# Routing attention into a cosine router on one core: early gathers held to their turns, four scatters moved behind the region, the last pair's groups summed in one visit

## The chip, the core and the metric

The kernel runs on one core of a Trainium2 chip. The metric is the time of one execution on the device in microseconds (us), as the median of several runs. The core has engines that each work through their own list of instructions in order: PE (TensorE; PEld is its weight load), DVE (VectorE), ACT (ScalarE), POOL (GpSimd) and SP (SyncE, which here only issues DMAs). They wait for each other by semaphores. All numbers below are of the kernel before the change.

## What is computed

```python
def attention(q, k, v, centroids):            # q, k, v: 4 x 8 x 768 x 64; centroids: 8 x 16 x 64
    q_assign = argmax(cosine(q, c), -1)       # each query and key belongs to one of 16 clusters
    k_assign = argmax(cosine(k, c), -1)
    mask = q_assign[:, :, :, None] == k_assign[:, :, None, :]
    scores = where(mask, q @ k.T / sqrt(64), -1e9)
    attn = exp(scores - max(scores))
    return (attn / (sum(attn) + 1e-9)) @ v

def router(x, expert_emb, tau, w1, w2):       # x: 3072 x 512; w1: 8 x 512 x 1024; w2: 8 x 1024 x 512
    logits = cosine(x, expert_emb) / tau
    expert_idx = argmax(logits, 1)
    gate = softmax(logits)[arange(N), expert_idx]
    for e in range(8):
        mask = expert_idx == e
        out[mask] = gate[mask, None] * (relu(x[mask] @ w1[e]) @ w2[e])

x = attention(...).transpose(0, 2, 1, 3).reshape(3072, 512)
out = router(x, ...)
```

Everything is float32. Each token goes to a single expert, so the tokens of one expert have to be gathered, multiplied, and scattered back.

## The kernel before

**Attention.** The 4 batches and 8 heads are worked off as 16 pairs n of two heads (four pairs to a batch, b and nb). A pair has two groups (the halves of the 768 queries), a group has six units, and one iteration `it` of the main loop (0 to 5 within a pair) does two units. For a unit, `scores` (line 571) multiplies a block of keys with the queries, together with a small product of one-hot cluster codes that does the masking; `expo` (582, ACT) makes `prob`; `attend` (593, PE) multiplies it with v, and DVE adds it up into `acc` (602, 612). The scores of a unit are issued one iteration ahead of its `attend`.

After a pair come its denominators and its x. `total` (643) multiplies `acc` with ones on PE, which sums over the keys. Called with two groups it uses tiles of 32 output rows and 192 columns, transposes the sums on DVE (660), takes the reciprocal of few elements (661) and lets POOL spread them with eight copies (664). Called with one group it uses 64 rows and 384 columns, and DVE takes the reciprocal of 128x384 directly (652). `divide` transposes the spread reciprocals back (675, two groups only) and makes `xT` (679). `rows` transposes xT (696) and stores it into the DRAM tensor `x_rows` with four DMAs from SP (703). All pairs but the last do this with both groups at once, in the next pair's iterations. The last pair calls each of `total`, `divide`, `rows` and `products` once for each group: the first group within the pair, the second in the tail behind it. `products` (722, PE) multiplies xT with the expert embeddings, `logits` (734, DVE) transposes the result, `choose` finds each token's expert, with a running sum `cumx` on POOL (776).

**Experts.** The tokens of one expert are cut into items. Four items, `E0[0]` to `E0[3]`, are "early": blocks of 128 tokens of earlier batches, whose tables are made during the last two batches. Behind them come the items of `later`, alternately "block" (128 tokens) and "sized" (160 to 272 tokens). For an item, POOL gathers the rows of x with four indirect DMAs (1144, one for each quarter), `turn_x` transposes them (1262 on DVE; 1269 with eviction 1272 on ACT for E0[0]), `hidden` multiplies by w1 in two halves of 16 matmuls (1386, evicted by ACT at 1393; sized items at 1293 and 1300), `result` multiplies by w2 (1426, evicted at 1437), and POOL scatters the rows to `out_dram` (1155). Early items also gather their gates (`fetch_gate`, tile gatein). The weights have two slots for w1 and two for w2; SP loads 2 MB at a time (1194), the first loads in halves of 1 MB.

**What sets the order.** Each engine's list is written out by hand: the instructions stand in the order in which the Python code issues them. The table `early` names, by batch, pair and iteration, what is put into the main loop. For the gathers of E0[1] and E0[2] it says:

```python
(3, 3, 2): lambda: early_lot(1, 2),
(3, 3, 3): lambda: early_lot(1, 1),
(3, 3, 4): lambda: early_lot(1, 1),
(3, 3, 5): lambda: early_lot(2, 1),
```

`early_lot(j, n, behind)` issues the next n gathers of item j. With `behind`, POOL first copies one element of that tile, so that the gathers behind it on POOL can't go before the tile is written. The calls in the loop have no `behind`; those in the tail copy an element of a `hT`.

The tail behind the main loop runs on PE in this order: products of the last pair's first group, half of E0[0]'s hidden, `total` of the second group, the other half, products of the second group, E0[1]'s hidden, `ranks` (858, 865), result of E0[0], and on.

In the last loop, over `later`, scatters and gathers lie in a list `queue` with a due item. `pump(n, behind)` issues the next n; `share` issues as many as are needed to have those that are due issued in time. Between the halves of the result of item LAST-2 stands `overflow()`, a region under `tc.If` (1732) that is run only if more blocks are needed than planned. The six scatters of the sized item LAST-3 are due at LAST-2, and are issued before and at this region.

Of the kernel before, what the change touches and what calls it, by code (L numbers as in the profile page):

```python
# [9 lines left out]
F32 = mybir.dt.float32  # L10
# [8 lines left out]
P = 128  # L19

SQ = 32
# [18 lines left out]
def kernel(  # L40
# [590 lines left out]
    def total(*gs):  # L631

        g = gs[0]
        d = gr[g]
        n = units[GU * g][0]
        G = len(gs)
        bk = misc()

        M, W = (D, HS) if G == 1 else (D // 2, HS // 2)
        for i in range(P // M):  # L640
            for k, g in enumerate(gs):
                c = i * W % HS
                nc.tensor.matmul(
                    bk[M * i : M * i + M, W * k : W * k + W],
                    lhsT=ones[:, 0:M],
                    rhs=gr[g]["acc"][:, i * W // HS, c : c + W],
                    start=True,
                    stop=True,
                )
        den = d["den"] = smp.tile([P, G, HS], F32, tag="den", name="den", bufs=1)  # L650
        if G == 1:
            nc.vector.reciprocal(den[:, 0], bk[:, 0:W])
            return


        U = W // SQ
        sums = smp.tile([P, G * U, SQ], F32, tag="sums", name="sums", bufs=1)
        inv = smp.tile([P, G, U], F32, tag="inv", name="inv", bufs=1)
        inv2 = d["inv2"] = smp.tile([P, G, 2, U], F32, tag="inv2", name="inv2", bufs=1)
        nc.vector.transpose(sums.rearrange("p g i -> p (g i)"), bk[:, 0 : G * W])  # L660
        nc.vector.reciprocal(inv.rearrange("p k u -> p (k u)"), sums[:, :, 0])  # L661
        for i in range(4):
            for to in (i, i ^ 1):
                nc.gpsimd.tensor_copy(  # L664
                    inv2[M * to : M * to + M, :, i % 2], inv[M * i : M * i + M]
                )

    def divide(*gs):
        n, hq, _ = units[GU * gs[0]]
        d = gr[gs[0]]  # L670
        G = len(gs)
        if hq == 0:
            xT[pairs[n]] = xp.tile([P, 2, HS], F32, tag="xT", name="xT", bufs=4)
        if G == 2:
            nc.vector.transpose(
                d["den"].rearrange("p k (u t) -> p (k u) t", t=SQ),
                bc(d["inv2"].rearrange("p k h u -> p (k h u)"), [P, G * HS // SQ, SQ], 2),
            )
        nc.vector.scalar_tensor_tensor(
            out=xT[pairs[n]][:, hq : hq + G],  # L680
            in0=ld[n]["o_sum"][:, hq : hq + G, 0:HS],
            scalar=ld[n]["o_sum"][:, hq, HS:HE],
            in1=d["den"],
            op0=ALU.add,
            op1=ALU.mult,
        )
        for g in gs:
            gr[g].clear()
# [680 lines left out]
    def flat(t):  # L1369
        return t.rearrange("p k w -> p (k w)")  # L1370

    def hidden(it, halves=(0, 1)):

        d = mo[it]
        for half in halves:
            if half == 0:
                d["hT"] = (
                    flat(szp.tile([P, KF, max(CAPS)], F32, tag="hTs", name="hTs", bufs=1))[:, 0:F]
                    if it.kind == "whole"
                    else mop.tile([P, F], F32, tag="hT", name="hT")  # L1380
                )
            f0 = 512 * half
            bk = psH.tile([P, 512], F32, tag="h_ps", name="h_ps")
            for m in range(0, 512, P):
                for c in range(KD):
                    nc.tensor.matmul(  # L1386
                        bk[:, m : m + P],
                        lhsT=w1s[it.slot][:, c, f0 + m : f0 + m + P],
                        rhs=d["xT"][:, P * c : P * c + P],
                        start=(c == 0),  # L1390
                        stop=(c == KD - 1),
                    )
            nc.scalar.activation(d["hT"][:, f0 : f0 + 512], bk, ACTF.Relu)  # L1393

    def result_last(it):

# [18 lines left out]
    def result(it, halves=(0, 1)):  # L1415
# [44 lines left out]
        (3, 2, 3): lambda: fetch(E0[0]),  # L1460
        (3, 2, 5): lambda: order_x(E0[0]),
        (3, 3, 1): pa.spread_pieces,
        (3, 3, 2): lambda: early_lot(1, 2),
        (3, 3, 3): lambda: early_lot(1, 1),
        (3, 3, 4): lambda: early_lot(1, 1),
        (3, 3, 5): lambda: early_lot(2, 1),
    }
    early_jobs = {}

    def early_lot(j, n, behind=None):  # L1470

        if j not in early_jobs:
            early_jobs[j] = fetches(E0[j])
        if behind is not None:
            nc.gpsimd.tensor_copy(pace, behind)
        for job in early_jobs[j][0:n]:
            job()
        del early_jobs[j][0:n]
# [81 lines left out]
    with tc.manual_schedule(engines=by_hand):  # L1560
        begin()
        for i in range(0, len(units), 2):
# [14 lines left out]
                begun()  # L1577
                continue
            between(n, it)
            if it == 4 and n == NP - 1:  # L1580
                divide(2 * n)
            b, nb = divmod(n, NHP)
            if (b, nb, it) in early:
                early[b, nb, it]()
# [12 lines left out]
                unite(2 * n)  # L1597
            elif it == 5:
                unite(2 * n + 1)
            if i + 2 == len(units):  # L1600
                rows(ngroups - 2)
                route[b][0](0)
            if it == 0 and n > 0:
                total(2 * n - 2, 2 * n - 1)
            if it == 0 and n > 0:
                piece(n + 1, "products")
            if (nb, it) == (0, 4) and b > 0:
                route[b - 1][0](0, 1)
            if it == 3 and n == NP - 1:
                total(2 * n)  # L1610
        at.close()
        mop = ctx.enter_context(tc.tile_pool(name="mop", bufs=2, **tile_waits))
        rtb = ctx.enter_context(tc.tile_pool(name="rtb", bufs=1, **tile_waits))
# [8 lines left out]
        pb = Places(1, rtb)  # L1622
        gates = gate_pieces(0, B - 1)
        gates[0]()
        early_lot(2, 1)
        logits(0)
        hidden(E0[0], (0,))
        turn_x(E0[1])
        early_lot(2, 2, mo[E0[0]]["hT"][0:1, 511:512])
        total(ngroups - 1)  # L1630
        divide(ngroups - 1)
        ato.close()
        psY = ctx.enter_context(tc.tile_pool(name="psY", bufs=1, space=PSUM, reuse_waits="tile"))
        rows(ngroups - 1)
        gates[1]()
        gates[2]()
        hidden(E0[0], (1,))
        turn_x(E0[2])
        gates[3]()
        early_lot(3, 2, mo[E0[0]]["hT"][0:1, F - 1 : F])  # L1640
        weights1(E0[2])
        read(0, NJ, P - SQ, P)
        products(1)
        hidden(E0[1], (0,))
        logits(1)
        choose()
        early_lot(3, 2, mo[E0[1]]["hT"][0:1, 511:512])
        hidden(E0[1], (1,))
        weights1(E0[3])
        pb.ranks()  # L1650
        pb.firsts()
        for it in E0:
            fetch_gate(it)
        result(E0[0], (0,))
        pb.dest(0)
        pb.dest(1)
        result(E0[0], (1,))
        weights2(E0[2])
        pb.hot_blocks()
# [97 lines left out]
        for i, it in enumerate(later):  # L1757
# [8 lines left out]
            made = None  # L1766
            if i > 0 and later[i - 1].kind == "sized":
                made = mo[later[i - 1]]["ys"][0:1, 0, 0:1]
                queue.extend((min(i + 1, LAST - 2), f) for f in sends(later[i - 1]))
            if 0 < i < LAST - 1 and later[i + 2].kind == "sized":  # L1770
                jobs_of(later[i + 2], i)
            for k in range(i + 2, i + 4):
# [8 lines left out]
                    weights2(later[i + 2])  # L1781
                sized_result(it, lambda g, x: share(i, 3 - g, x) if g < 3 else None)
            elif i < LAST:
                share(i, 3, made)
                hidden(it, (0,))
                share(i, 2, mo[it]["hT"][0:1, 511:512])
                hidden(it, (1,))
                share(i, 1, mo[it]["hT"][0:1, F - 1 : F])
                if i == 0:
                    turn_x(later[1])  # L1790
                    pb.gates(slot_gates)
# [59 lines left out]
```

## Time and profile before

| what | us |
|---|---|
| median of 3 runs (698.12, 696.0, 698.7) | 698.12 |
| the profiled execution, whole | 695.11 |
| its span | 693.0 |
| clock of PE granted, mean | 0.998 |
| busy: DVE, ACT, POOL | 382.8, 262.2, 275.6 |
| POOL gathers (L1144), 56 | 56.8 |
| POOL scatters (L1155), 56 | 55.8 |
| moved by DMA | 135.55 MB, mean 196 GB/s |

The profile is of one execution. Times in it are counted from the start of its span; the execution as a whole took 2.1 us more. A line of the timeline gives start, duration, engine, source line, operation, output and inputs, and in brackets how long the engine sat idle before and what ended it. A line of the waits gives the total, the count and the longest. In the windows the DMA share is the mean busy share of the 16 DMA engines, and a number in brackets is a count of instructions. Rows of matmuls can lie over each other, as matmuls are pipelined: the distance to the next start is the better measure of what a group costs. Some matmul records can be missing.

The last attention pair lies at about 304 to 325 us, the tail with the early items from there to about 370, the region at 650.5, and the last scatter is issued at 688.69.

### The profile page before, as it was taken

What the parts mean: (1) busy time and instruction counts of PE and PEld (TensorE: products, weight loads), DVE (VectorE), ACT (ScalarE), POOL (GpSimd) and SP (SyncE); (2) the same over time, 40 slices, a digit from 0 to 9 for tenths busy, and PEclk for the clock granted to TensorE, in tenths of its full rate; (3) what the DMA queues carried; (4) which work ended last, traced back from release to release, by engine and by line L of the source; (5) the groups of instructions that cost most, each with busy time, mean ns of one, the idle gap of its engine ahead of it and who ended that gap; (6) DMA issues with size and microseconds to landing.
All of it is one profiled execution on the core that took longest, in us unless ns stands there. A gap on an engine that the chain in (4) does not pass through costs nothing. (4 is left out here: it accounts for less than half of the span.)

```text
span 693.0 us, 16339 instructions
## 1 busy us (share of the span) xinstructions
PE 682.6 (99%) x6521; PEld 460.4 (66%) x6521; DVE 382.8 (55%) x673; ACT 262.2 (38%) x444; POOL 275.6 (40%) x505
## 2 busy tenths in 40 slices
PE   8999999999999999999999999999999999999987
PEld 4544444444544444445866678888979797979785
DVE  6898998999899999997674122140301203030310
ACT  6665665576566765574242120101010101111011
POOL 2221222322131222343526343676756465647403
PEclk9999999999999999999999999999999999999999
DMA  9757755776678687689699957457787686878630
GB/s 147 121 82 116 114 100 86 153 141 106 108 131 163 139 147 142 171 209 292 175 311 388 372 189 268 147 175 279 281 282 280 202 301 231 306 249 310 242 133 33
DMA packets 244956, 135.55 MB, mean 196 GB/s; under 512 B 208640, under 2 KB 208642, under 8 KB 244876
## 3 DMA queue, kind: packets, MB, share of 16 engines
q1 hardware_dynamic: 238540, 121.29, 65.0%
q0 software_dynamic: 6160, 13.12, 5.6%
q8 instruction: 53, 0.87, 0.5%
q14 instruction: 27, 0.22, 0.1%
q10 hardware_dynamic: 176, 0.05, 0.0%
HBM read 115.93 MB, written 13.12 MB: 186 GB/s over the span
## 5 line engine op out<-in xcount | busy, mean ns | idle before, releaser
L582 ACT ACTIVATE prob<-s_ps 128x768 f32<-128x768 f32 x192 | 154.0, 814 | 104.7 <-PE s_ps L571 98.6
L571 PE MATMUL s_ps<-qT,kT 64*64 64x384 f32 x1536 | 156.9, 483 | 0.0
L593 PE MATMUL o_ps<-prob,v 64*64 64x385 f32 x1536 | 143.3, 484 | 0.6 <-issue 0.6
L612 DVE TENSOR_TENSOR acc<-acc,prob 128x768 f32<-128x768 f32 x128 | 121.5, 949 | 8.9 <-ACT prob L582 0.5
L593 PEld LDWEIGHTS o_ps<-prob,v 64*64 64x64 f32 x1536 | 58.6, 133 | 66.4 <-issue 58.1
L1340 DVE STREAM_TRANSPOSE ys<-y_ps 128x256 f32<-128x256 f32 (+4 forms) x16 | 6.1, 403 | 154.4 <-PE y_ps L1331 126.6
L1386 PEld LDWEIGHTS h_ps<-xTm,w1s 128*128 128x128 f32 x768 | 87.3, 192 | 2.0 <-issue 1.6
L1386 PE MATMUL h_ps<-xTm,w1s 128*128 128x128 f32 x768 | 88.3, 276 | 0.0
L571 PEld LDWEIGHTS s_ps<-qT,kT 64*64 64x64 f32 x1536 | 55.7, 133 | 35.9 <-issue 31.7
L1426 PE MATMUL y_ps<-w2s,hT 128*128 128x512 f32 x176 | 77.8, 594 | 0.3 <-PEq L1732 0.3
L1293 PE MATMUL h_ps<-xTs,w1s 128*128 128x272 f32 (+7 forms) x384 | 72.9, 346 | 1.8 <-ACT hTs L1300 1.8
L627 POOL COPY behind<-acc 1x1 f32<-1x1 f32 x30 | 6.7, 222 | 168.3 <-DVE acc L612 159.5
L1293 PEld LDWEIGHTS h_ps<-xTs,w1s 128*128 128x128 f32 x384 | 66.7, 190 | 8.6 <-issue 2.9
L1393 ACT ACTIVATE hT<-h_ps 128x512 f32<-128x512 f32 x24 | 14.3, 596 | 147.3 <-PE h_ps L1386 107.8
L1155 POOL DMA_INDIRECT out_dram<-ys,spidx x56 | 55.8, 997 | 33.9 <-issue 19.5
L571 PE MATMUL s_ps<-hot 64*64 64x384 bf16 x768 | 64.6, 325 | 0.1
L1144 POOL DMA_INDIRECT xs<-x_rows,gpidx x56 | 56.8, 1013 | 18.7 <-issue 18.7
L1426 PEld LDWEIGHTS y_ps<-w2s,hT 128*128 128x128 f32 x176 | 32.5, 190 | 37.4 <-issue 36.3
L571 PEld LDWEIGHTS <-hot 64*64 64x64 bf16 x768 | 24.2, 106 | 43.4 <-issue 41.5
L1331 PE MATMUL y_ps<-hTs,w2o 128*128 128x272 f32 (+7 forms) x256 | 48.0, 346 | 0.0
L1331 PE MATMUL misc<-hTs,w2o 128*128 128x272 f32 (+7 forms) x256 | 48.0, 346 | 0.0
L664 POOL COPY inv<-inv 32x12 f32<-32x12 f32 x120 | 31.5, 262 | 36.8 <-DVE inv L661 32.6
(285 smaller groups left out, 740.3 us busy)
## 6 DMA issues: line engine op xcount, KB each, us to landing
w1s<-in_moe_w_dram SPq DMA_DIRECT2D x18, 2048.0 KB
w2s<-in_moe_w_dram SPq DMA_DIRECT2D x18, 2048.0 KB
q<-in_q_dram SPq DMA_DIRECT2D x64, 96.0 KB
k<-in_k_dram SPq DMA_DIRECT2D x64, 96.0 KB
v<-in_v_dram SPq DMA_DIRECT2D x120, 48.0 KB
x_rows<-xb SPq DMA_DIRECT2D x60, 96.0 KB
xr<-x_rows SPq DMA_DIRECT2D x9, 512.0 KB
w1s<-in_moe_w_dram SPq DMA_DIRECT2D x4, 1024.0 KB
```

The costliest lines, as they stand in the source:

```text
L571: nc.tensor.matmul(s_ps[D * half : D * half + D, h, 0:HS], lhsT=l[rows, half], rhs=r[rows], start=part == (1 if len(parts) < 2 else 0), st ...
L582: nc.scalar.activation(d["prob"][:, :, 0:HS], d["s_ps"][:, :, 0:HS], ACTF.Exp, scale=scale)
L593: nc.tensor.matmul(g["o_ps"][D * h : D * h + D, half, 0:HE], lhsT=ld[n]["v"][keys, j, h], rhs=d["prob"][keys, h, 0:HE], start=(j == 0), st ...
L612: nc.vector.tensor_tensor(g["acc"], g["acc"], d["prob"][:, :, 0:HS], ALU.add)
L664: nc.gpsimd.tensor_copy(inv2[M * to : M * to + M, :, i % 2], inv[M * i : M * i + M])
L1144: nc.gpsimd.indirect_dma_start(out=to, out_offset=None, in_=of, in_offset=bass.IndirectOffsetOnAxis(ap=at, axis=0), bounds_check=n - 1, oo ...
L1155: inst = nc.gpsimd.indirect_dma_start(out=to, out_offset=bass.IndirectOffsetOnAxis(ap=at, axis=0), in_=of, in_offset=None, bounds_check=n - 1,
L1293: nc.tensor.matmul(bk, lhsT=w1s[it.slot][:, c, P * f : P * f + P], rhs=d["xT"][:, c, 0:C], start=(c == 0), stop=(c == KD - 1),)
L1331: nc.tensor.matmul(bks[g][:, 0:C], lhsT=d["w2"][:, f, P * g : P * g + P], rhs=d["hT"][:, f, 0:C], start=(f == 0), stop=(f == KF - 1),)
L1386: nc.tensor.matmul(bk[:, m : m + P], lhsT=w1s[it.slot][:, c, f0 + m : f0 + m + P], rhs=d["xT"][:, P * c : P * c + P], start=(c == 0), stop ...
L1393: nc.scalar.activation(d["hT"][:, f0 : f0 + 512], bk, ACTF.Relu)
L1426: nc.tensor.matmul(bk, lhsT=d["hT"][:, P * c : P * c + P], rhs=w2s[it.slot][:, c], start=(c == 0), stop=(c == KF - 1),)
```

## The change

There are four parts.

1. The last pair's two groups are summed, divided, stored and multiplied once, together, as in the other pairs; all of it stands in the tail. `total` loses its form for one group. `hidden` gets a `span`, so that the products stand in the middle of the first half of E0[1]'s hidden.
2. The gathers of E0[1] in the last pair are one to an iteration, each behind a POOL copy of an element of the `prob` of that iteration's first unit (`ahead`). Those of E0[2] stand in the tail: two behind E0[0]'s transposed x, two behind its hT. Those of E0[3] stand behind `choose` (two) and behind `pb.first` (two). The gates of E0[2] and E0[3] are gathered behind `pb.d`.
3. In SP's order, the stores of the gate rows and the load of E0[2]'s w1 come ahead of the last pair's stores of x_rows.
4. In the last loop two of the six scatters of item LAST-3 are issued before the region; the others are due at LAST-1 and are issued one at a time within its `sized_hidden`.

```diff
--- before.py
+++ after.py
@@ -636,7 +636,7 @@
         G = len(gs)
         bk = misc()
 
-        M, W = (D, HS) if G == 1 else (D // 2, HS // 2)
+        M, W = D // 2, HS // 2
         for i in range(P // M):
             for k, g in enumerate(gs):
                 c = i * W % HS
@@ -647,11 +647,7 @@
                     start=True,
                     stop=True,
                 )
-        den = d["den"] = smp.tile([P, G, HS], F32, tag="den", name="den", bufs=1)
-        if G == 1:
-            nc.vector.reciprocal(den[:, 0], bk[:, 0:W])
-            return
-
+        d["den"] = smp.tile([P, G, HS], F32, tag="den", name="den", bufs=1)
 
         U = W // SQ
         sums = smp.tile([P, G * U, SQ], F32, tag="sums", name="sums", bufs=1)
@@ -671,11 +667,10 @@
         G = len(gs)
         if hq == 0:
             xT[pairs[n]] = xp.tile([P, 2, HS], F32, tag="xT", name="xT", bufs=4)
-        if G == 2:
-            nc.vector.transpose(
-                d["den"].rearrange("p k (u t) -> p (k u) t", t=SQ),
-                bc(d["inv2"].rearrange("p k h u -> p (k h u)"), [P, G * HS // SQ, SQ], 2),
-            )
+        nc.vector.transpose(
+            d["den"].rearrange("p k (u t) -> p (k u) t", t=SQ),
+            bc(d["inv2"].rearrange("p k h u -> p (k h u)"), [P, G * HS // SQ, SQ], 2),
+        )
         nc.vector.scalar_tensor_tensor(
             out=xT[pairs[n]][:, hq : hq + G],
             in0=ld[n]["o_sum"][:, hq : hq + G, 0:HS],
@@ -1369,19 +1364,21 @@
     def flat(t):
         return t.rearrange("p k w -> p (k w)")
 
-    def hidden(it, halves=(0, 1)):
+    def hidden(it, halves=(0, 1), span=(0, 512)):
 
         d = mo[it]
         for half in halves:
-            if half == 0:
+            if half == 0 and span[0] == 0:
                 d["hT"] = (
                     flat(szp.tile([P, KF, max(CAPS)], F32, tag="hTs", name="hTs", bufs=1))[:, 0:F]
                     if it.kind == "whole"
                     else mop.tile([P, F], F32, tag="hT", name="hT")
                 )
             f0 = 512 * half
-            bk = psH.tile([P, 512], F32, tag="h_ps", name="h_ps")
-            for m in range(0, 512, P):
+            if span[0] == 0:
+                d["h_ps"] = psH.tile([P, 512], F32, tag="h_ps", name="h_ps")
+            bk = d["h_ps"]
+            for m in range(*span, P):
                 for c in range(KD):
                     nc.tensor.matmul(
                         bk[:, m : m + P],
@@ -1390,7 +1387,8 @@
                         start=(c == 0),
                         stop=(c == KD - 1),
                     )
-            nc.scalar.activation(d["hT"][:, f0 : f0 + 512], bk, ACTF.Relu)
+            if span[1] == 512:
+                nc.scalar.activation(d["hT"][:, f0 : f0 + 512], bk, ACTF.Relu)
 
     def result_last(it):
 
@@ -1460,11 +1458,13 @@
         (3, 2, 3): lambda: fetch(E0[0]),
         (3, 2, 5): lambda: order_x(E0[0]),
         (3, 3, 1): pa.spread_pieces,
-        (3, 3, 2): lambda: early_lot(1, 2),
-        (3, 3, 3): lambda: early_lot(1, 1),
-        (3, 3, 4): lambda: early_lot(1, 1),
-        (3, 3, 5): lambda: early_lot(2, 1),
+        **{(3, 3, it): lambda it=it: early_lot(1, 1, ahead(3, 3, it)) for it in (2, 3, 4, 5)},
     }
+
+    def ahead(b, nb, it):
+
+        return un[2 * (NJ * (NHP * b + nb) + it)]["prob"][0:1, 0, 0:1]
+
     early_jobs = {}
 
     def early_lot(j, n, behind=None):
@@ -1472,7 +1472,8 @@
         if j not in early_jobs:
             early_jobs[j] = fetches(E0[j])
         if behind is not None:
-            nc.gpsimd.tensor_copy(pace, behind)
+            at = smp.tile([1, 1], F32, tag="behind", name="behind", bufs=1)
+            nc.gpsimd.tensor_copy(at, behind)
         for job in early_jobs[j][0:n]:
             job()
         del early_jobs[j][0:n]
@@ -1577,8 +1578,6 @@
                 begun()
                 continue
             between(n, it)
-            if it == 4 and n == NP - 1:
-                divide(2 * n)
             b, nb = divmod(n, NHP)
             if (b, nb, it) in early:
                 early[b, nb, it]()
@@ -1597,17 +1596,12 @@
                 unite(2 * n)
             elif it == 5:
                 unite(2 * n + 1)
-            if i + 2 == len(units):
-                rows(ngroups - 2)
-                route[b][0](0)
             if it == 0 and n > 0:
                 total(2 * n - 2, 2 * n - 1)
             if it == 0 and n > 0:
                 piece(n + 1, "products")
             if (nb, it) == (0, 4) and b > 0:
                 route[b - 1][0](0, 1)
-            if it == 3 and n == NP - 1:
-                total(2 * n)
         at.close()
         mop = ctx.enter_context(tc.tile_pool(name="mop", bufs=2, **tile_waits))
         rtb = ctx.enter_context(tc.tile_pool(name="rtb", bufs=1, **tile_waits))
@@ -1622,38 +1616,41 @@
         pb = Places(1, rtb)
         gates = gate_pieces(0, B - 1)
         gates[0]()
-        early_lot(2, 1)
-        logits(0)
+        early_lot(2, 2, mo[E0[0]]["xT"][0:1, 0:1])
+        turn_x(E0[1])
         hidden(E0[0], (0,))
-        turn_x(E0[1])
-        early_lot(2, 2, mo[E0[0]]["hT"][0:1, 511:512])
-        total(ngroups - 1)
-        divide(ngroups - 1)
-        ato.close()
-        psY = ctx.enter_context(tc.tile_pool(name="psY", bufs=1, space=PSUM, reuse_waits="tile"))
-        rows(ngroups - 1)
+        total(ngroups - 2, ngroups - 1)
         gates[1]()
         gates[2]()
         hidden(E0[0], (1,))
+        gates[3]()
+        weights1(E0[2])
+        divide(ngroups - 2, ngroups - 1)
+        ato.close()
+        psY = ctx.enter_context(tc.tile_pool(name="psY", bufs=1, space=PSUM, reuse_waits="tile"))
+        rows(ngroups - 2, ngroups - 1)
+        read(0, NJ, P - SQ, P)
+        hidden(E0[1], (0,), (0, 256))
+        products(0, 1)
+        hidden(E0[1], (0,), (256, 512))
+        early_lot(2, 2, mo[E0[0]]["hT"][0:1, F - 1 : F])
+        logits(0, 1)
+        choose()
         turn_x(E0[2])
-        gates[3]()
-        early_lot(3, 2, mo[E0[0]]["hT"][0:1, F - 1 : F])
-        weights1(E0[2])
-        read(0, NJ, P - SQ, P)
-        products(1)
-        hidden(E0[1], (0,))
-        logits(1)
-        choose()
-        early_lot(3, 2, mo[E0[1]]["hT"][0:1, 511:512])
+        early_lot(3, 2)
         hidden(E0[1], (1,))
         weights1(E0[3])
         pb.ranks()
         pb.firsts()
-        for it in E0:
+        for it in E0[0:2]:
             fetch_gate(it)
+        early_lot(3, 2, pb.first[0:1, 0:1])
         result(E0[0], (0,))
         pb.dest(0)
         pb.dest(1)
+        nc.gpsimd.tensor_copy(pace, pb.d[0:1, 0:1])
+        for it in E0[2:]:
+            fetch_gate(it)
         result(E0[0], (1,))
         weights2(E0[2])
         pb.hot_blocks()
@@ -1766,7 +1763,8 @@
             made = None
             if i > 0 and later[i - 1].kind == "sized":
                 made = mo[later[i - 1]]["ys"][0:1, 0, 0:1]
-                queue.extend((min(i + 1, LAST - 2), f) for f in sends(later[i - 1]))
+                due = LAST - 1 if i == LAST - 2 else min(i + 1, LAST - 2)
+                queue.extend((due, f) for f in sends(later[i - 1]))
             if 0 < i < LAST - 1 and later[i + 2].kind == "sized":
                 jobs_of(later[i + 2], i)
             for k in range(i + 2, i + 4):
@@ -1781,11 +1779,16 @@
                     weights2(later[i + 2])
                 sized_result(it, lambda g, x: share(i, 3 - g, x) if g < 3 else None)
             elif i < LAST:
-                share(i, 3, made)
+                if i == LAST - 2:
+                    pump(2, made)
+                else:
+                    share(i, 3, made)
                 hidden(it, (0,))
-                share(i, 2, mo[it]["hT"][0:1, 511:512])
+                if i < LAST - 2:
+                    share(i, 2, mo[it]["hT"][0:1, 511:512])
                 hidden(it, (1,))
-                share(i, 1, mo[it]["hT"][0:1, F - 1 : F])
+                if i < LAST - 2:
+                    share(i, 1, mo[it]["hT"][0:1, F - 1 : F])
                 if i == 0:
                     turn_x(later[1])
                     pb.gates(slot_gates)
```

## The prediction

> **What bounds the kernel now.** The page's first part comes first:
>
> ```profile
> PE 682.6 (99%) x6521; PEld 460.4 (66%) x6521; DVE 382.8 (55%) x673; ACT 262.2 (38%) x444; POOL 275.6 (40%) x505
> ```
>
> PE works for 682.6 of 693.0 us, so time is won only where PE has fewer matmuls, waits less, or works faster at the same matmuls. The waits of PE say how little the second can give:
>
> ```profile
> PE h_ps L1293 <- ACT hTs L1300: 1.8, 1, 1.8
> PE x_ps L1269 <- ACT prob L582: 0.9, 1, 0.9
> PE o_ps L593 <- issue: 0.6, 1, 0.6
> ```
>
> The other waits lie at the start, or are 0.3 us. The 1.8 us wait is read in the timeline near the end, and in the chain of waits:
>
> ```profile
> 650.49 0.98 POOL L1155 DMA_INDIRECT out_dram<-ys,spidx  x1 [0.57 <-issue]
> 651.77 0.97 POOL L1155 DMA_INDIRECT out_dram<-ys,spidx  x1 [0.30 <-DVE xTm L1262]
> 659.68 0.69 ACT L1437 ACTIVATE y<-y_ps,slot_gates 128x512 f32<-128x512 f32 x1 [10.07 <-DMA xin<-x_rows,gpidx]
> 660.61 3.53 PE L1293 MATMUL h_ps<-xTs,w1s 128*128 128x160 f32 x24 [1.77 <-ACT hTs L1300]
> ```
> ```profile
> 644.70 14.67 DMA out_dram<-ys,spidx
> ```
>
> Six scatters are issued from 643.36 to 651.77, the last two at the `tc.If` of `overflow`. ACT is idle for 10.07 us although the y_ps that it evicts was done at 654.33, where the next matmuls begin. The chain ties its start to a scatter: POOL passes the branch only when its DMAs have landed, and ACT's eviction waits behind POOL. PE runs out of evicted banks and loses 1.77 us. The other two waits belong to a longer loss at the end of attention, which the timeline shows:
>
> ```profile
> 307.52 4.53 POOL L664 COPY inv<-inv 32x12 f32<-32x12 f32 x8 [2.06 <-DVE inv L661]
> 317.08 1.52 PE L571 MATMUL s_ps<-qT,kT 64*64 64x384 f32 x8
> 318.10 2.31 PE L593 MATMUL o_ps<-prob,v 64*64 64x385 f32 x13
> 318.85 2.56 DVE L652 RECIPROCAL den<-misc 128x384 f32<-128x384 f32 x1 [2.54 <-PE s_ps L571]
> 321.06 1.51 ACT L582 ACTIVATE prob<-s_ps 128x768 f32<-128x768 f32 x2 [3.77 <-remote]
> 322.71 0.63 PE L1269 MATMUL x_ps<-ident,rows 128*128 128x128 f32 x4 [0.86 <-ACT prob L582]
> ```
>
> A group of eight L571 matmuls took 0.81 us at 313.26 and 1.52 at 317.08; thirteen of L593 took 2.31 where sixteen took 1.46 at 313.90. ACT and DVE idle for results of PE that arrive late. Windows cut at 1 us show what is different there:
>
> ```profile
> core 0: us, PE busy (x) PEld busy (x) DVE busy (x) ACT busy (x) POOL busy (x), PEclk, DMA share, GB/s
> 300.00:310.00 10.00, 10.00 (x148) 5.00 (x144) 9.07 (x13) 6.91 (x12) 4.08 (x8) 1.00 0.89 252
> 316.00:317.00 1.00, 1.00 (x18) 0.61 (x18) 0.31 (x1) 1.00 (x2) 0.70 (x2) 1.00 1.02 391
> 318.00:319.00 1.00, 1.00 (x9) 0.43 (x10) 0.15 (x1) 0.00 (x0) 0.89 (x1) 1.00 1.06 406
> 320.00:321.00 1.00, 0.43 (x5) 0.13 (x2) 1.00 (x1) 0.00 (x0) 0.19 (x1) 1.00 1.04 385
> ```
>
> In 318 to 319 PE retired 9 matmuls, against 14.8 per us in 300 to 310, at full clock. The DMA engines are full (share above 1): three weight halves of 1 MB (issued 311.22 to 312.8), four x_rows stores (from 315.50), and six early gathers (312.32 to 320.19). With usual durations the attention would have ended near 320.9 (320.1, plus 0.80 for the L643 at 315.29) and not at 324.72: about 3.8 us are lost.
>
> **What the Trainium skill says.** SBUF — State Buffer, "Who interferes with whom": PE and ACT never wait on anyone, and DMA never contends with an engine. The trace shows PE slowed beside full DMA engines without naming a contender, so it does not settle that. The same section has an exclusive lock between GpSimd and DVE instructions with two SBUF inputs. The trace agrees: the eight L664 copies took 4.53 us at 307.52, beside DVE's adds, and 2.23 without them. TensorE: Matmul & The Clock Gate, "Part 3: Packing small matmuls — row/col tiling" lets matmuls with few output columns run side by side. The trace agrees, see the first sum. DMA: Bandwidth & Descriptors, "Latency and other measured facts" has HBM latency rise from 0.2 us to 2 us under load; gathers here took 2.6 to 3.1 us from issue to landing on quiet queues (330.77, 332.10, 336.43) and 5.6 to 6.6 in 312 to 320.
>
> **The change part by part.**
> *Matmuls.* A single L643 group (64 wide, four) took 0.80 us to the next start, 315.29 to 316.09, twice (329.29 too). Sixteen 32-wide ones for two groups also took 0.80 (305.64 to 306.44). One call in place of two saves 0.80. The products of one half took 0.80, twice (324.72, 333.85), those of both halves 1.44 (103.64 to 105.08): 1.60 − 1.44 = 0.16. Sum 0.96 us, all on PE, which is the path: sure.
>
> *Scatters.* Four of six move behind the region. The first two were issued at 643.36 and 644.70 and had landed by 646.9, before the region at 650.5; POOL then has nothing to wait for there and ACT evicts soon after 654.3. 1.77 us go. Moved, each costs POOL a pace copy of 0.18 and an issue of about 1.0 (rows above), 4 × 1.5 = 6 us, in a stretch where POOL sat idle 13.82 us before 675.44. They land at latest some 7 us after issue (650.49 landed at 656.9), by about 671, before the five last sends from 675.44. What is late next is nothing I can find: h_ps follows the matmuls with 0.8 us ACT idle. With the first part: 2.73 us.
>
> *Early gathers.* Gates of one POOL copy (0.18, and about 0.5 to the issue) hold each of four gathers to its unit. Three go at about the old times, because copies and issues fill POOL to 312.3 anyway; the fourth goes at 318 or later. The two of the third item go behind the eviction of the first item's x, the end of attention. The four x_rows stores at 315.50 are gone as well. So of 4.9 MB in the full stretch (3 MB weights, 1.5 MB gathers of 256 KB each, 0.38 MB rows) 3.8 MB are left. How much of the 3.8 us comes back no row shows. Bounds: 0, if the weights do it; 3.8, if gathers or rows do. Near 400 GB/s at 303 to 311, without gathers, PE was not slowed, which speaks for the gathers; at 492 to 498, in the experts, gathers at 398 GB/s did not slow it either, which speaks against them. I take the middle, 1.9. A loss here I exclude: less is asked of the DMA engines.
>
> *The chain in the tail.* Instead of a direct reciprocal (2.56 us on DVE, twice) both groups take: transposed sums and reciprocal (0.58, 0.23), eight POOL copies (2.23), transpose (0.98), division (1.02), and then products. Let t be the end of attention on PE. PE then has half a hidden (3.77), L643 (0.80), half a hidden (3.77), eight matmuls (1.88); products' first twelve matmuls need no xT of the last pair, the thirteenth does at t + 10.8. xT is ready at t + 4.6 + 0.9 + 2.23 + 2.0 = 9.7, with waits between engines about 10.1, if the copies wait for nothing. In the instruction order of the changed kernel the third copy waits for all six early gathers to land, and the two of the third item are issued only at about t and t + 1.3; DVE also has two expert transposes (0.7 each) ahead. Landed at L, xT comes at L + 4.0. On quiet queues L = t + 1.3 + 2.6 = t + 3.9 and nothing is late; with the longest landing, 6.6, L = t + 7.9 and PE waits 1.1. If the copies take 4.53 beside DVE, the wait is 1.3. Bounds 0 to 1.3, taken 0.5.
>
> *Moved DMAs and gates, with no price.* SP now issues the gate rows and the third item's w1s (waits for the first item's hidden, t + 8.3) ahead of rows; rows waits for xb anyway, and the weights land about t + 17.8 (8.1 us as at 339.17) against a need at t + 24. The xr reads come later by some us, but feed norms long after. The fourth item's gathers (two after choose, two after firsts) stand before POOL's later gathers and cost PE nothing while gatein (t + 23.5) precedes its eviction (t + 24.0). This cover is thin: half a us. POOL's rr22b keeps about 1.5 us.
>
> The sum: −0.96 − 1.77 − 1.9 + 0.5 = −4.1. The profiled execution took 695.11 (span 693.0 and 2.1 around it): 691.0. The runs shown have a median of 698.12, three above the profiled one; from that median 694.0.
>
> **Rivals.** Forecast: part of the slow stretch comes back, 694.0.
> A: the slow stretch belongs to the weight loads, which stay. 2.73 − 0.5 = 2.2 saved: 695.9. For it: the slowing begins as the weights land (317.0 to 323.5). Against: the same loads earlier did not slow PE.
> B: it belongs to gathers or rows: 2.73 + 3.8 − 0.5 = 6.0, 692.1. Against: gathers 1 to 3 still fall among the loads.
> C, the other side: the third POOL copy waits for the gathers. It makes PE wait once L passes t + 6.8. With no recovery the 2.73 is eaten at L = t + 9.5, a landing of 8.2 us, and at t + 13.0 the kernel is 3.5 slower: 701.6. The longest landing seen is 6.6, and 6.7 for gatein; but a late DVE also holds ranks, tokens and all later due times with it, whose slack is 2 us or less.
>
> **How the numbers follow.** 0.5% (3.5 us) is what a measurement of this kernel can tell from no change. Chances: forecast 0.40, A 0.30, B 0.20, C 0.10. Faster: B, most of the forecast's (0.35) and 0.02 of A, 0.57. Slower: 0.08 of C. Same: the rest, 0.35. The range goes from B's 692.1, less the runs' spread of about 1.4, to 699.0, where A meets that spread and C begins.
>
> **What would show it.** L643 once with 16 records, and L722 once with 192-wide, 0.96 less PE busy; no 1.77 before L1293 at the region, ACT's eviction right after 654 of the old clock; the L571 groups after 314 at 0.81 and no 3.77 idle of ACT (B), or 1.5 as before (A). A PE wait inside L722 of 0 to 1.3 us is the chain; one of over 4 is C. The prediction is wrong if the tail shows a new PE wait longer than 2.7 us, or a second one in ranks, tokens or y_ps.

## The result, and the profile after

The changed kernel took 690.69 us (median of 6, 690.27 to 692.96), the kernel before 698.49 (6 runs, 696.0 to 699.32): ratio 0.9897, 95% interval 0.9877 to 0.9917, 7.8 us faster. (Ratios below are to the kernel before in the same series, each with its 95% interval.) The two profiled executions differ by less: spans of 688.3 and 693.0, because the profiled execution of before was quicker (695.11) than all its timed ones (696.0 to 699.32). The kernel before also takes 690 on one chip and 695 to 698 on the others; the experiments had to find out why.

The page's first part and the waits of PE, after:

```profile
PE 680.4 (99%) x6497; PEld 460.1 (67%) x6497; DVE 380.8 (55%) x671; ACT 262.8 (38%) x444; POOL 282.9 (41%) x520
```
```profile
PE idle_ps L235 <- DVE epsc L258: 1.1, 1, 1.1
PE misc L1035 <- DVE used L965: 0.9, 1, 0.9
PE y_ps L1424 <- PEq L1729: 0.3, 1, 0.3
```

The three waits shown of before are gone, and one of 0.9 us is new. (Lines are those of the changed file: L1288 was L1293, L1383 was L1386, L1139 was L1144.) The end of attention in the timeline, and its windows of 1 us:

```profile
316.63 0.81 PE L571 MATMUL s_ps<-qT,kT 64*64 64x384 f32 x8
317.27 1.46 PE L593 MATMUL o_ps<-prob,v 64*64 64x385 f32 x16
320.71 3.84 PE L1383 MATMUL h_ps<-xTm,w1s 128*128 128x128 f32 x32
324.48 0.88 PE L643 MATMUL misc<-acc,ones 128*32 128x192 f32 x16
```
```profile
core 0: us, PE busy (x) PEld busy (x) DVE busy (x) ACT busy (x) POOL busy (x), PEclk, DMA share, GB/s
316.00:317.00 1.00, 1.00 (x20) 0.45 (x16) 0.90 (x2) 0.66 (x3) 0.84 (x2) 1.00 0.97 350
317.00:318.00 1.00, 1.00 (x20) 0.46 (x16) 0.90 (x2) 1.00 (x2) 1.00 (x1) 1.00 1.05 410
318.00:319.00 1.00, 1.00 (x15) 0.40 (x8) 0.90 (x2) 0.94 (x3) 0.93 (x2) 1.00 1.03 373
```

The DMA engines are as full as before (share 0.97 to 1.05, 350 to 410 GB/s), yet PE retires 15 to 20 matmuls per us and the groups take their usual 0.81 and 1.46. So in this kernel full DMA engines do not slow PE by themselves.

Marks in the order of PE's work show where the time comes from (start times of the rows, before and after):

| mark | before | after | gain so far |
|---|---|---|---|
| `total` of the pair before the last (L643) | 305.64 | 306.10 | −0.46 |
| first hidden of the tail (L1386, now L1383) | 325.52 | 320.71 | 4.81 |
| ranks (L858, now L853) | 341.90 | 337.74 | 4.16 |
| tokens (L1040, now L1035) | 359.54 | 356.46 | 3.08 |
| first L1293 at the region (now L1288) | 654.33 | 651.37 | 2.96 |
| second L1293 | 660.61 | 655.72 | 4.89 |
| end of the span | 693.0 | 688.3 | 4.7 |

From the first mark to ranks 4.62 us are gained. Of these 0.96 are the saved matmuls, so 3.7 are the slow stretch; from there to tokens 1.08 are lost, and at the region 1.93 gained.

### The profile page after: what moved, and what is told of

Read it like the earlier page. It is cut to its first block, busy times and chain, and to the rows that moved or that the text cites. A ratio compares the mean times of both kernels' runs of the same rounds, so it can differ in the third digit from the quotient of the medians.

```text
span 688.3 us, 16309 instructions
## 1 busy us (share of the span) xinstructions
PE 680.4 (99%) x6497; PEld 460.1 (67%) x6497; DVE 380.8 (55%) x671; ACT 262.8 (38%) x444; POOL 282.9 (41%) x520
## 5 line engine op out<-in xcount | busy, mean ns | idle before, releaser
L571 PE MATMUL s_ps<-qT,kT 64*64 64x384 f32 x1536 | 156.2, 483 | 0.0
L593 PE MATMUL o_ps<-prob,v 64*64 64x385 f32 x1536 | 141.5, 484 | 0.0
L1383 PEld LDWEIGHTS h_ps<-xTm,w1s 128*128 128x128 f32 x768 | 87.4, 192 | 2.3 <-issue 2.2
L1383 PE MATMUL h_ps<-xTm,w1s 128*128 128x128 f32 x768 | 88.4, 276 | 0.0
L571 PEld LDWEIGHTS s_ps<-qT,kT 64*64 64x64 f32 x1536 | 55.4, 133 | 35.8 <-issue 31.8
L1288 PE MATMUL h_ps<-xTs,w1s 128*128 128x272 f32 (+7 forms) x384 | 72.8, 346 | 0.0
L1288 PEld LDWEIGHTS h_ps<-xTs,w1s 128*128 128x128 f32 x384 | 66.7, 190 | 6.6 <-issue 2.9
L571 PE MATMUL s_ps<-hot 64*64 64x384 bf16 x768 | 64.5, 325 | 0.1
L1139 POOL DMA_INDIRECT xs<-x_rows,gpidx x56 | 56.7, 1013 | 18.7 <-issue 18.7
L571 PEld LDWEIGHTS <-hot 64*64 64x64 bf16 x768 | 24.1, 106 | 42.7 <-issue 41.2
L660 POOL COPY inv<-inv 32x12 f32<-32x12 f32 x128 | 33.0, 258 | 41.3 <-DVE inv L657 33.4
```

Source lines behind the costliest of these rows:

```text
L571: nc.tensor.matmul(s_ps[D * half : D * half + D, h, 0:HS], lhsT=l[rows, half], rhs=r[rows], start=part == (1 if len(parts) < 2 else 0), st ...
L593: nc.tensor.matmul(g["o_ps"][D * h : D * h + D, half, 0:HE], lhsT=ld[n]["v"][keys, j, h], rhs=d["prob"][keys, h, 0:HE], start=(j == 0), st ...
L660: nc.gpsimd.tensor_copy(inv2[M * to : M * to + M, :, i % 2], inv[M * i : M * i + M])
L1139: nc.gpsimd.indirect_dma_start(out=to, out_offset=None, in_=of, in_offset=bass.IndirectOffsetOnAxis(ap=at, axis=0), bounds_check=n - 1, oo ...
L1288: nc.tensor.matmul(bk, lhsT=w1s[it.slot][:, c, P * f : P * f + P], rhs=d["xT"][:, c, 0:C], start=(c == 0), stop=(c == KD - 1),)
L1383: nc.tensor.matmul(bk[:, m : m + P], lhsT=w1s[it.slot][:, c, f0 + m : f0 + m + P], rhs=d["xT"][:, P * c : P * c + P], start=(c == 0), stop ...
```

## The experiments

There are four series, each on another chip, and each with runs of the kernel before beside it.

**First series: the parts alone.** The gathers alone:

```diff
-        (3, 3, 2): lambda: early_lot(1, 2),
-        (3, 3, 3): lambda: early_lot(1, 1),
-        (3, 3, 4): lambda: early_lot(1, 1),
-        (3, 3, 5): lambda: early_lot(2, 1),
+        **{(3, 3, it): lambda it=it: early_lot(1, 1, ahead(3, 3, it)) for it in (2, 3, 4, 5)},
...
-        early_lot(2, 1)
+        early_lot(2, 2, mo[E0[0]]["xT"][0:1, 0:1])
         logits(0)
```

> The kernel before with one part alone: the four gathers of E0[1] each behind the prob of its iteration, those of E0[2] behind xT and hT of E0[0]. Theory G (the slow stretch of PE at 314 to 322 comes from gathers issued back to back): the stretch is gone, L571 stays at 0.81 for 8, ratio to before 0.990 to 0.9945. Theory S (it comes from the single group's total and divide inside the loop): the stretch stays, ratio 0.999 to 1.001.

The merged sums alone: the changed kernel with these lines taken back, and those of the scatters.

> The kernel after with the early gathers of the loop unheld again and the six scatters where they were before: the merged sums alone, with the new order of the tail. Theory S: the slow stretch is gone, 3.7 + 0.96 us or more saved, ratio 0.990 to 0.9935. Theory G: the stretch stays slow, 0.96 us saved, ratio 0.998 to 0.9995.

The scatters alone (the last part of the diff, in the kernel before):

> The kernel before with the scatters alone moved behind the region. Both theories: the 1.77 us wait of PE before L1293 at the region goes, ratio 0.9975. If the executions without a profile wait longer at the region than the profiled one (their median is 3 us above it), ratio down to 0.993.

And the kernel before, unchanged, for a second profile:

> The kernel before, for a second profile. If the slow stretch belongs to the order of the work, it shows at the same place with 3 to 7 us lost; if it is chance, its place or size differs.

Measured: gathers 690.01 (ratio 0.9999, 0.9991 to 1.0008), sums 689.79 (0.9999, 0.9990 to 1.0007), scatters 689.88 (1.000, 0.9991 to 1.0008), each against 690.01 for the kernel before (33 runs, 689.5 to 690.92). No theory had all three: here the kernel before is as quick as the changed one was in the first comparison. The delays that the gathers and the scatters were to remove are not there, and of the sums' 0.96 us only 0.2 show, with a new wait of 0.6 for rr22b (L1035) in their profile. The whole change was not run on this chip. The second profile of the kernel before, in the timeline:

```profile
317.14 0.81 PE L571 MATMUL s_ps<-qT,kT 64*64 64x384 f32 x8
317.22 1.62 ACT L582 ACTIVATE prob<-s_ps 128x768 f32<-128x768 f32 x2 [1.60 <-PE s_ps L571]
651.36 0.69 ACT L1437 ACTIVATE y<-y_ps,slot_gates 128x512 f32<-128x512 f32 x1 [7.15 <-DMA xin<-x_rows,gpidx]
655.16 3.42 PE L1293 MATMUL h_ps<-xTs,w1s 128*128 128x160 f32 x24
```

The six gathers are issued back to back from 312.37, the same weights are under way, but the L571 group at 317.14 takes 0.81 and PE does not wait at the region. Laid beside the first profile, PE's starts agree (325.52 − 322.01 = 3.51 behind the stretch, and still 654.33 − 650.82 = 3.51 ahead of the second L1293), except at two places: the stretch, and the region (660.61 − 655.16 = 5.45). At both, in the first profile, an engine that waited for PE began late although PE's row had ended: ACT's prob at 315.87 for scores that ended at 314.07, and ACT's hT at 649.01 for a hidden that ended at 647.08. The lines of that first profile:

```profile
313.26 0.81 PE L571 MATMUL s_ps<-qT,kT 64*64 64x384 f32 x8
313.66 1.32 POOL L1144 DMA_INDIRECT xin<-x_rows,early_i  x1 [0.31 <-issue]
315.29 1.00 POOL L1144 DMA_INDIRECT xin<-x_rows,early_i  x1 [0.30 <-issue]
315.87 0.81 ACT L582 ACTIVATE prob<-s_ps 128x768 f32<-128x768 f32 x1 [1.37 <-remote]
639.77 7.31 PE L1386 MATMUL h_ps<-xTm,w1s 128*128 128x128 f32 x64
649.01 0.60 ACT L1393 ACTIVATE hT<-h_ps 128x512 f32<-128x512 f32 x1 [4.87 <-remote]
```

Beside both, POOL was issuing indirect DMAs one right after another. This gave a new theory, P: where the delay shows, PE's signals (the semaphore increments by which PE tells the others that a group is done) arrive 1 to 2 us late while POOL issues indirect DMAs back to back.

**Second series: the changed kernel again, the new wait, and the region.**

> The changed kernel itself. Theory D (the first comparison's 7.8 us are delays that only its device showed: PE's signals came late there in the kernel before): here the two differ by less than 1 us, ratio 0.9985 to 1.0005, because the 0.96 us of matmuls are eaten by the wait of PE for POOL's rr22b (0.6 to 0.9). Theory K (the order of the kernel before is at fault by itself): ratio 0.988 to 0.992.

The gates of the third and fourth item behind POOL's part of `hot_blocks`:

```diff
-        nc.gpsimd.tensor_copy(pace, pb.d[0:1, 0:1])
-        for it in E0[2:]:
-            fetch_gate(it)
         result(E0[0], (1,))
         weights2(E0[2])
         pb.hot_blocks()
         pb.hot_rows(0, 1)
+        for it in E0[2:]:
+            fetch_gate(it)
```

> The changed kernel, with the gate gathers of E0[2] and E0[3] moved from ahead of rr22b on POOL to behind it. If PE's wait in front of L1035 is POOL's (gathers queued ahead of rr22b): the wait of 0.6 to 0.9 us goes and this is 0.6 to 0.9 faster than the changed kernel, ratio to before 0.997 to 0.999. If it is DVE's: as the changed kernel.

Ten small copies on POOL between hT and the last two scatters ahead of the region, in the kernel before; and the same copies with the four scatters moved:

```diff
                 hidden(it, (1,))
+                if i == LAST - 2:
+                    for _ in range(10):
+                        nc.gpsimd.tensor_copy(pace, mo[it]["hT"][0:1, F - 1 : F])
                 share(i, 1, mo[it]["hT"][0:1, F - 1 : F])
```

> The kernel before with ten more one-element copies on POOL (1.8 us and more) between hT of item LAST-2 and the last two scatters ahead of the region: it sets the delay that the first profile showed there. If POOL's wait for its scatters at the region holds ACT and so PE, PE waits 1.5 to 4 us in front of L1293 and the time rises by as much: ratio 1.002 to 1.006. If not, 1.000.

> The same ten copies at the same place, in the kernel before with the scatters alone moved behind the region. POOL has nothing of its own to wait for there: no wait of PE in front of L1293, ratio 0.999 to 1.001. If the copies themselves cost (POOL late at the region), as in the run without the moved scatters.

Measured, against 695.07 for the kernel before (14 runs, 694.0 to 697.43): changed kernel 690.04 (0.9926, 0.9912 to 0.9940); gates later 689.02 (0.9910, 0.9894 to 0.9925); the copies in the kernel before 700.90 (1.0075, 1.0052 to 1.0098); with the scatters moved 693.45 (0.9978, 0.9966 to 0.9989). On this chip the kernel before has its delays (the first run with copies, whose code differs from it only at the region, shows ACT's 1.37 and 3.77 us of idle time at the end of attention again), and the changed kernel takes what it took in the first comparison. Neither D nor K is right as put: the delays depend on the chip, but where they occur it is the order of the kernel before that lets them in.

The copies show the region, first in the kernel before, then with the scatters moved (timelines):

```profile
649.37 1.11 POOL L1155 DMA_INDIRECT out_dram<-ys,spidx  x1 [0.30 <-issue]
651.08 0.60 ACT L1393 ACTIVATE hT<-h_ps 128x512 f32<-128x512 f32 x1 [4.88 <-remote]
651.81 2.29 POOL L1790 COPY pace<-hT 1x1 f32<-1x1 f32 x10 [1.33 <-ACT hT L1393]
664.89 0.69 ACT L1437 ACTIVATE y<-y_ps,slot_gates 128x512 f32<-128x512 f32 x1 [13.21 <-DMA xin<-x_rows,gpidx]
665.82 4.93 PE L1293 MATMUL h_ps<-xTs,w1s 128*128 128x160 f32 x24 [4.93 <-ACT hTs L1300]
```
```profile
648.93 0.60 ACT L1393 ACTIVATE hT<-h_ps 128x512 f32<-128x512 f32 x1 [2.98 <-PE h_ps L1386]
649.65 2.73 POOL L1795 COPY pace<-hT 1x1 f32<-1x1 f32 x10 [2.16 <-ACT hT L1393]
656.38 0.69 ACT L1437 ACTIVATE y<-y_ps,slot_gates 128x512 f32<-128x512 f32 x1 [6.86 <-PE y_ps L1426]
660.48 3.42 PE L1293 MATMUL h_ps<-xTs,w1s 128*128 128x160 f32 x24
```

2.29 us of copies ahead of two scatters raise PE's wait at the region to 4.93, from 1.77 in the first profile; with the scatters behind the region 2.73 us of copies cost no wait. So the scatters' landing is what ACT waits for at the branch: in the first profile the last of them landed at 657.79 and POOL's wait for it ended at 657.81. Both forecasts of time missed. With the copies the time rose by 5.8 us, not by 1.5 to 4: of the 6.6 us between the spans of this profiled execution and the first one, 3.2 are the longer wait, 1.4 the slower L1293 group behind it (4.93 against 3.53), and some 2 lie ahead of the region. With the scatters moved the kernel is 1.6 us faster than before, not equal to it, because the forecast left out that the move takes the old wait of 1.77 away too. The scatters alone were not run on a chip with delays. The pair shows P too: the hidden's rows end at 649.14 (644.73 + 4.41) in the first and at 648.89 (644.82 + 4.07) in the second. ACT begins 1.94 us behind that in the first, where POOL issues scatters at 648.08 and 649.37, and 0.04 behind it in the second, where POOL issues none. The ten copies come after, so they are not the cause.

Gates later, POOL and PE:

```profile
349.02 1.47 POOL L1019 TENSOR_TENSOR rr22b<-bm22b,tok_lo 128x528 bf16<-128x528 bf16 x1
354.97 0.76 PE L1035 MATMUL misc<-rr22b,ohrb 128*128 128x44 bf16 x24
```

In the changed kernel rr22b stood behind the two gate gathers as well (two gathers of E0[3] and a scatter stand ahead of it in both):

```profile
350.29 3.68 POOL L1139 DMA_INDIRECT gatein<-gate_rows,gidx  x1 [0.30 <-issue]
354.27 1.03 POOL L1150 DMA_INDIRECT out_dram<-y,sidx  x1 [0.30 <-ACT junk L750]
355.32 1.08 POOL L1019 TENSOR_TENSOR rr22b<-bm22b,tok_lo 128x528 bf16<-128x528 bf16 x1
356.46 0.76 PE L1035 MATMUL misc<-rr22b,ohrb 128*128 128x44 bf16 x24 [0.92 <-DVE used L965]
```

rr22b ends at 356.40, 0.06 us before PE starts; the wait, which the view puts down to DVE, is POOL's. With the gates later it is gone, and the kernel is 1.0 us faster than the changed one in the same series (689.02 against 690.04, and their runs do not overlap). It is the fastest of this study. (The ratio forecast for it, 0.997 to 0.999, had taken theory D for true.)

**Third series: which part cures the stretch.** Gathers and merged sums, each alone, once more:

> The held gathers alone once more, where the kernel before shows its slow stretch (its own time beside this one tells: near 690 it does not). Theory P (PE's signals arrive 1 to 2 us late while POOL issues indirect DMAs one after another): held to their turns the gathers leave PE's signals alone, L571 stays at 0.81 after 314, 3.5 to 5.5 us saved, ratio 0.992 to 0.995. Theory S (the single group's sum in the loop): the stretch stays, ratio 1.000.

> The merged sums alone once more, with the gathers of the loop back to back as before. Theory P: ACT's prob is still late (1.7 us) beside the gathers and most of the stretch stays slow; 0 to 2.5 us saved, ratio 0.9965 to 1.000. Theory S: the stretch is gone, ratio 0.992 to 0.995.

Measured against 696.04 (22 runs, 695.53 to 700.16): gathers 692.30 (0.9947, 0.9928 to 0.9965), sums 694.38 (0.9971, 0.9957 to 0.9985). The gathers alone, ACT and PE:

```profile
317.35 1.57 ACT L582 ACTIVATE prob<-s_ps 128x768 f32<-128x768 f32 x2 [1.23 <-POOL behind L1478]
317.87 1.46 PE L593 MATMUL o_ps<-prob,v 64*64 64x385 f32 x16
```

The sums alone:

```profile
316.16 0.81 ACT L582 ACTIVATE prob<-s_ps 128x768 f32<-128x768 f32 x1 [1.42 <-remote]
317.02 0.36 PE L571 MATMUL s_ps<-hot 64*64 64x384 bf16 x4 [0.61 <-ACT prob L582]
320.20 0.63 PE L1264 MATMUL x_ps<-ident,rows 128*128 128x128 f32 x4 [0.73 <-ACT prob L582]
```

Held gathers leave the stretch at its usual speed with `total` still in the loop; 3.7 us come back. With the sums merged and the gathers back to back, ACT's prob is as late as in the first profile (idle 1.42, there 1.37). PE loses about 1.7 us instead of 3.5 (L1264 against the same row of the first series: 320.20 − 318.51), probably because DVE's late reciprocal is no longer in its way, which no run tells apart. Theory S falls as the cause, P holds.

**Fourth series: spacing alone, and the change without the merged sums.**

```diff
         for job in early_jobs[j][0:n]:
+            if behind is None:
+                for _ in range(6):
+                    at = smp.tile([1, 1], F32, tag="behind", name="behind", bufs=1)
+                    nc.gpsimd.tensor_copy(at, ident[0:1, 0:1])
             job()
```

> The kernel before with six one-element copies of a constant on POOL ahead of each of the six early gathers in and right behind the loop: spaced by about 2.3 us instead of 1.3, held to nothing. If it is the issue back to back that delays PE's signals, spacing alone cures most of the stretch: ratio 0.994 to 0.996 where the kernel before shows the stretch. If the gathers have to stand behind the prob of their turn, the stretch stays: 0.999 to 1.001.

> The held gathers and the moved scatters together, without the merged sums. If the two gains add (3.7 and 1.8 us where the kernel before shows both delays): ratio 0.9915 to 0.993, and within 0.4 us of the changed kernel, whose saved matmuls (0.96) are eaten by the wait for rr22b (0.9). If the merged sums bring their 0.96: 1 us slower than the changed kernel.

Measured against 695.50 (11 runs, 694.83 to 696.37): spaced 698.23 (1.0044, 1.0030 to 1.0058), held gathers and moved scatters 689.76 (0.9918, 0.9905 to 0.9930). The spaced one is slower, but not for the stretch:

```profile
318.09 1.46 PE L593 MATMUL o_ps<-prob,v 64*64 64x385 f32 x16
323.62 1.18 POOL L1144 DMA_INDIRECT xin<-x_rows,early_i  x1 [0.54 <-issue]
331.31 0.71 DVE L1262 STREAM_TRANSPOSE xTm<-xin 128x512 f32<-128x512 f32 x1 [6.29 <-DMA xin<-x_rows,early_i]
```
```profile
PE misc L722 <- DVE xT L679: 3.8, 1, 3.8
PE h_ps L1293 <- ACT hTs L1300: 1.9, 1, 1.9
```

The stretch is at its usual speed, although nothing holds the gathers to a turn: the gaps are enough. (Here only two gathers fall into the stretch, at 314.66 and 318.42. In the changed kernel four do, at 312.89, 314.76, 316.98 and 319.09, about 2 us apart and not 1.3, and the stretch is at its usual speed too.) But the copies took up to 3.63 us for six beside DVE's adds, the fourth gather went at 326.69, and DVE had to wait for it ahead of the last pair's xT: PE lost 3.8 us there, more than the stretch gave. The kernel without the merged sums is as fast as the changed one was on the chip of the second series (0.9918 and 0.9926; the intervals overlap).

**All of PE's signals.** The traces also record when each increment of PE's semaphore took effect. Matched in order with the PE rows that give them, these records test theory P over the whole kernel. In the first profile PE gives 435 such signals. For 314 of them POOL ran no indirect DMA in the 1.3 us before the end of PE's row: all took effect within 0.07 us of it. Of the other 121, 77 were on time, and 44 came 0.4 to 3.9 us late or have no record of their own. (The latest are two in the stretch, at 2.7 and 3.9 us, so the 1 to 2 us of theory P are too few there.) The recorded signals of ACT, DVE and POOL are at most 0.03 us late. In the second profile, on the chip without delays, all 435 signals of PE are within 0.07 us, though POOL's issues stand beside 123. The changed kernel has as many late or unrecorded signals as the kernel before, 45 of 434: it does not make them rarer, but keeps them away from the two places where PE soon needs the answer.

## Why the prediction was right, and where not

The direction was right, and 690.69 lies just at the low end of the range (692.1 less about 1.4). The size was off: 4.1 us forecast, 7.8 in the first comparison and 5.0 in the second series. There was luck in it: most of the gain is delays that not every chip has, which the prediction did not know of.

- **Matmuls, 0.96.** As predicted: L643 once with 16 records, L717 once with 1.43 to the next start. It is all eaten later, which the prediction did not have.
- **Scatters, 1.77.** Right in mechanism and size: 1.93 between the marks, and the pair with ten copies shows both the wait and its cure. What the prediction did not have is why the last two scatters were late: they stand behind the hT whose signal came 1.9 us late, and on the chip without delays the kernel before has no wait here.
- **The early gathers, taken 1.9 of 0 to 3.8.** This term was mis-sized: 3.7 came back, the whole, as in rival B (the second profile puts the loss at 3.5, not 3.8). Its reason failed as well. The prediction had PE slowed by full DMA engines, and counted the x_rows stores at 315.50 among what goes. Those belong to the pair before the last and stand at 315.95 in the changed kernel; the DMA share is the same in both. What goes is the delay of PE's signals beside POOL's issues. In the prediction's own windows the sign was ACT's idle time put down to "remote" and DVE's late reciprocal, with PE's rows long ended: signals late, not matmuls slow at first.
- **The chain in the tail, taken 0.5 of 0 to 1.3.** No wait: the copies took 1.81 at 326.91, xT was ready at 330.88, 10.2 us behind the end of attention at 320.71, where PE needs it at 10.8. It was closer than forecast: xT came 5.5 us behind the landing of E0[1]'s gathers (at 325.40, when DVE's transpose of them starts) and not 4.0, because operations of the gates on DVE (L786 to L801) went in between. Rival C did not come about here, but the spaced gathers are its price: the transposes of E0[1], which wait for gathers, stand ahead of the sums on DVE, and 3.8 us of PE were lost.
- **POOL's rr22b, "about 1.5 us" of slack.** This is the other step that failed. The two late gates were costed against their own need only. They took POOL 1.50 and 3.68 us, and with the scatter behind them made rr22b 0.92 late: the price of the split gates. This wait stands in tokens, one of the places that the prediction named as a sign of being wrong if a second new wait came there; it is the only new one, as the chain brought none. It cancels the saved matmuls, with which the run without merged sums agrees.
- **The sum.** With the measured terms 0.96 + 1.93 + 3.7 − 1.1 = 5.5, less 0.5 by which the changed kernel was behind at the first mark, which lies ahead of the change, and 0.3 elsewhere: the 4.7 of the spans. The second series gave 5.0. What the kernel before lost beyond that in the first comparison, some 3 us, no profile shows, as its profiled execution was quicker than its others; that stays open.

The Trainium skill's SBUF — State Buffer, "Who interferes with whom", says that PE never waits on anyone. The traces agree: on the chip of the first series PE ran at full speed beside the same gathers and loads (0.81 us for the L571 group at 317.14). What is late here is not PE's own work but the word of it.

Shown is that gathers held or spaced, and scatters taken away, remove the late starts at these places, that with POOL's issues the eviction behind the same row is 1.94 us late and without them 0.04, and that no signal of PE away from such issues is late. Not shown is how an issue of POOL delays a signal of PE, nor why one of the four chips of the experiments is free of it.

## What to carry to other kernels

Where an engine idles for a result whose row has ended long before, look at what the other engines issue in that time before blaming bandwidth; then compare with a run in which the same transfers are under way. A gap on POOL between indirect DMAs can be worth more than the early start of the transfer, but what waits for the last of them on an in-order engine sets how far they may be spread. And before a small piece is put ahead on a queue, count the whole queue behind it: here the 0.96 us of saved matmuls went into two gate gathers that nobody needed yet.

## What the runs showed of the hardware that was not expected

- The same program took 690.0 us on one chip and 695.1, 695.5 and 696.0 on three others. The difference lies at two places of some us; elsewhere PE's starts in the two profiles of the kernel before agree within 0.15 us. On one of the three the change measured 0.7% (0.9926); on the first chip each of its parts alone measured nothing.
- Where it occurs, the delay is repeatable: ACT's idle time ahead of the second prob was 1.37 in the first profile and 1.42 on another chip, and the delay of the hT ahead of the region 1.93 (649.01 − 647.08) and 1.94.
- 2.29 us of one-element copies on POOL turned into 3.2 us more of waiting for PE at the branch than in the first profile, beside scatters that were now issued 2.2 and 3.5 us behind the weight load of 652.70 (at 654.90 and 656.19); in the first profile they went 0.15 ahead of and 1.1 behind theirs (650.49 and 651.77 against 650.64). The scatter at 650.49 took 6.4 us to land (656.86). On the chip without delays they went 2.0 and 0.6 ahead of the load (645.09 and 646.55 against 647.13) and landed in 2.4 and 2.9 us.
- In the first profile 44 of PE's 435 signals were late or unrecorded, all of them beside indirect DMAs of POOL; on the chip without delays none was, in the same program.
